# Attention and MoE on one core: a seven-product second matmul in another form, shared sums on VectorE or GpSimd, 32-bit turns of K and Q, added exponentials, and a re-planned order

## The chip, the cores and the metric

The kernel runs on one core of a Trainium2 chip. The time is device microseconds of an execution; before the change, three runs gave a median of 414.13 us (413.87 to 414.46). A profile comes from one execution under the hardware profiler. Engines are named as in the profile: PE is TensorE (PEld its weight loads), DVE is VectorE, ACT is ScalarE, POOL is GpSimd, SP is the queue that issues most stores.

## The reference

```python
# q, k, v: [8 batches, 12 heads, 448 tokens, 64], fp32
scores = q @ k.T / sqrt(64)                 # per batch and head
attn = softmax(scores)
attn_out = attn @ v
# heads side by side: x is [3584 tokens, 768]
h = x @ w_in                                # w_in [768, 2048]
g = h * sigmoid(h)
out = g @ w_out                             # w_out [2048, 768], out fp32
```

All matmul operands are rounded to fp16 in SBUF; sums are fp32 in PSUM.

## The kernel before

**Tiles and units.** A unit is one batch and one group of four heads; the first batch is cut in two pieces of queries, so there are 27 units (6 for batch 0, 3 for each of the others). For each unit GpSimd's queue issues loads of K, Q and V that turn fp32 into fp16 on the way. VectorE transposes 32x32 blocks of K and Q (`turn_k`, L279; `turn_q`, L290). Even and odd halves of the head dimension are separate slices, so that each score product contracts 32 rows, and four heads stand in four row groups of the PE array side by side.

**Attention.** `scores` (L303) writes a chunk of keys for two pairs of heads into two PSUM pairs of banks, ScalarE takes the exponential into an E buffer (`expo`, L340; nine buffers). Keys are in four chunks; from the fifth unit on, two units share their last chunk, 64 rows each (`scores_rest`). `attend` (L356) multiplies E with a matrix of ones (part 0, the denominators) and with two halves of V (parts 1 and 2), four heads in four column groups side by side; for a pair of units it does three chunks of each with 128 rows, and then both units' shares of the last chunk with 64 rows, eight abreast. VectorE inverts the denominators (`inverse`, L392 to L401) and normalises (`norm`, L409) into `xT`.

**First MoE matmul.** `ffn1` (L423), 16 row blocks of six products for each batch, then tanh on ScalarE (L434) and `gate` on VectorE (L470), which gives the gated rows `G` (with `X` for one tile that spans two batches).

**Second MoE matmul.** Token tiles of 128 are taken in pairs (`qd`, 14 pairs). For 13 pairs the 2x2 block product is made from seven block products in place of eight, each of eight matmuls (`product`, L514). Combinations of `w_out` blocks are made once (`combine_w`, L460), combinations of gated rows for each pair (`combine_g`, L504, all on VectorE). Two products share a PSUM bank by accumulation; the rest of the sums are six VectorE operations and three ScalarE copies for each pair (L567 to L581). The first pair is done plainly (`plain`, L528). Results leave by `store` (L562), four DMAs for each half tile.

**Order.** Nothing is scheduled by a compiler. A planner inside the kernel (`Order`, `Op`) runs a small clock with assumed durations, and emits each engine's instructions in the order in which it started them. Each engine then works its list strictly in order; semaphores hold real dependencies. TensorE takes scores when the pace allows, weighted sums when all exponentials of a unit are there, and else items of the MoE list. GpSimd's list holds nothing but DMA issues: `od.load` appends them in a fixed sequence. Here it is at the start, after the first batch's K, Q and V:

```python
plan_w_in(0, DFF // 4)
...
plan_w_in(DFF // 2, DFF)
plan_k(1, 1)
plan_q(NB0 + 1)
plan_w_out(0)
plan_k(1, 2)
plan_q(NB0 + 2)
for hg in range(NG):
    plan_v(1, hg, hg + 1)
plan_w_out(1)
```

Until there is real work, TensorE multiplies zeros (`run_zeros`, L1077) [...].

Of the kernel before, what the change touches and what calls it, by code (L numbers as in the profile page):

```python
# [1 line left out]

# [13 lines left out]

SWITCH = 0.094
PE_OUT = 0.20
HOP = 0.10
DMA_RATE = 0.37  # L20
DMA_TAIL = 1.0

# [5 lines left out]
def act(n):  # L28
    return n * 0.000833 + 0.093


class Ring:
# [5 lines left out]
    def can(self, n, now):  # L38
        return len(self.free) >= n and heapq.nsmallest(n, self.free)[-1] <= now

    def when(self, n):
        return heapq.nsmallest(n, self.free)[-1] if len(self.free) >= n else None

    def take(self, n=1):
        for _ in range(n):
            heapq.heappop(self.free)

    def give(self, at):
        heapq.heappush(self.free, at)
# [13 lines left out]
class Op:  # L63


    def __init__(self, eng, busy, emit, deps=(), bias=0.0, tail=HOP, then=None):
        self.eng, self.busy, self.emit = eng, busy, emit
        self.deps, self.bias, self.tail, self.then = list(deps), bias, tail, then
        self.done = None
        self.half = False  # L70
# [5 lines left out]
class Order:  # L76


    def __init__(self):
        self.now = 0.0  # L80
        self.free = {"PE": 1.2, "ACT": 2.1, "DVE": 1.2, "POOL": 1.2}
        self.wait = {"ACT": [], "DVE": []}
        self.pool = []
        self.dma_free = 0.0
        self.out = []
        self.mode = None
        self.busy = {e: 0.0 for e in self.free}
# [8 lines left out]
    def start(self, op):  # L96
        self.emit(op.emit)
        self.free[op.eng] = self.now + op.busy
        self.busy[op.eng] += op.busy
        op.done = self.now + op.busy + op.tail  # L100
        if op.then:
            op.then(op.done)
# [7 lines left out]
    def load(self, mb, emit, ring=None, gate=None):  # L110
        op = Op("POOL", 0.58, emit)
        self.pool.append((op, mb, ring, gate))
        return op

    def step(self):

        soon = []
        for eng in ("ACT", "DVE"):
            if self.free[eng] > self.now:
                soon.append(self.free[eng])  # L120
                continue
            best = None
            for op in self.wait[eng]:
                at = op.ready()
                if at is None:
                    continue
                if at > self.now:
                    soon.append(at)
                elif best is None or at + op.bias < best[0]:
                    best = (at + op.bias, op)  # L130
            if best:
                self.wait[eng].remove(best[1])
                self.start(best[1])
                soon.append(self.free[eng])
        if self.free["POOL"] > self.now:
            soon.append(self.free["POOL"])
        elif self.pool:
            op, mb, ring, gate = self.pool[0]
            at = 0.0
            if ring is not None:  # L140
                at = ring.when(1)
            if at is not None and gate is not None:
                g = gate()
                at = None if g is None else max(at, g)
            if at is not None and at <= self.now:
                self.pool.pop(0)
                if ring is not None:
                    ring.take()
# [10 lines left out]
def kernel(  # L159
# [24 lines left out]
    NFF = DFF // 128  # L184
    NDC = DM // 128
    NT = 2 * S // 128
    OH = DM // 2
    PACE = 2.6
    LONE = NG + 1
    PIECES = ((0, 7), (7, TPP))  # L190
    NE, NXT = 9, 18
    NSG, NTMP, NOST = 3, 3, 6
# [11 lines left out]
    ones = const.tile([128, 32], FP16, name="ones")  # L204
    nc.vector.memset(ones, 1.0)
# [3 lines left out]
    w_out_t = const.tile([128, NFF, DM], FP16, name="w_out_t")  # L209

    rawk, rawq, KT, QT, VT, E, acc, rdn_t, xT, g_t, ost_t = ({} for _ in range(11))
    sT_t, inv_t = {}, {}
    pS_t = {}
# [4 lines left out]
    def load_k(b, hg):  # L222
        t = sb.tile([128, TPP, 2, 32], FP16, name=f"rk_{b}_{hg}", tag="rk", bufs=2)
        nc.gpsimd.dma_start(out=t, in_=group_of(k, b, hg))  # L224
        rawk[(b, hg)] = t

    def load_q(n):
        b, hg, g0, g1 = units[n]
        t = sb.tile([128, g1 - g0, 2, 32], FP16, name=f"rq_{n}", tag="rq", bufs=3)
# [3 lines left out]
    def form(b, hg):  # L233
        n = NG * b + hg
        return "lone" if n < LONE else ("low", "high")[(n - LONE) % 2]


    def load_v(b, hg0, hg1, x):
        if b not in VT:
            VT[b] = sb.tile([128, NH, NCH, D], FP16, name=f"V_{b}", tag="V", bufs=2)  # L240
        hs = slice(HG * hg0, HG * hg1)
        first, count = X_TOK[form(b, hg0)][x]
        nc.gpsimd.dma_start(  # L243
            out=VT[b][32 * x : 32 * (x + 1), hs, 0:count, :],
# [4 lines left out]

# [15 lines left out]
    def turn_k(b, hg, e):  # L265
        t = rawk[(b, hg)]
        if e == 0:
            KT[(b, hg)] = sb.tile(
                [128, 2, NCH, 4, 32], FP16, name=f"KT_{b}_{hg}", tag="KT", bufs=3
            )  # L270
        kt = KT[(b, hg)]
        toks = X_TOK[form(b, hg)]
        x = 0
        while x < 4:
            first, count = toks[x]
            y = x + 1
            while y < 4 and toks[y][1] == count:
                y += 1
            nc.vector.transpose(  # L279
                out=kt[:, e].rearrange("p c x i -> p x c i")[:, x:y, 0:count],  # L280
                in_=t[:, first : first + count * (y - x), e, :].rearrange(
# [5 lines left out]
    def turn_q(n):  # L287
        b, hg, g0, g1 = units[n]
        qt = sb.tile([128, 2, g1 - g0, 32], FP16, name=f"QT_{n}", tag="QT", bufs=3)
        nc.vector.transpose(out=qt.rearrange("p e g i -> p g e i"), in_=rawq[n])  # L290
        QT[n] = qt

    def score_banks(n, w, ys):
        for y in ys:
            pS_t[(n, w, y)] = ps.tile(
                [128, 2, 512], FP32, name=f"s_{n}_{w}_{y}", tag="s", bufs=2
            )

    def score(pS, n, c, e, h, x0, x1, p0):
        b, hg, g0, g1 = units[n]  # L300
        nq = 32 * (g1 - g0)
        at = nq * (c % per_burst(n))
        nc.tensor.matmul(  # L303
            out=pS[p0 : p0 + 32 * (x1 - x0), h % 2, at : at + nq],
            lhsT=KT[(b, hg)][32 * h : 32 * (h + 1), e, c, x0:x1, :],
            rhs=QT[n][32 * h : 32 * (h + 1), e],
            start=(e == 0),
            stop=(e == 1),
        )


    def per_burst(n):
        return 2 if units[n][0] == 0 else 1

    def scores(n, w, ys):
        score_banks(n, w, ys)
        for c in range(per_burst(n) * w, per_burst(n) * (w + 1)):
            for e in range(2):
                for y in ys:
                    for h in (2 * y, 2 * y + 1):  # L320
                        score(pS_t[(n, w, y)], n, c, e, h, 0, rows_of(n, c) // 32, 0)


    def scores_rest(n):
        score_banks(n, 3, (0, 1))
        for e in range(2):
            for h in range(HG):
                pS = pS_t[(n, 3, h // 2)]
                score(pS, n, 3, e, h, 0, 2, 0)
                score(pS, n + 1, 3, e, h, 2, 4, 64)  # L330

    def rows_of(n, c):
        return KROWS[c] if form(*units[n][:2]) == "lone" else 128

    def expo(n, w, y):
        kr = rows_of(n, w * per_burst(n))
        nk = 32 * (units[n][3] - units[n][2]) * per_burst(n)
        if (n, w) not in E:
            E[(n, w)] = sb.tile([128, HG, S], FP16, name=f"E_{n}_{w}", tag="E", bufs=NE)
        nc.scalar.activation(  # L340
            out=E[(n, w)][0:kr, 2 * y : 2 * y + 2, 0:nk],
            in_=pS_t[(n, w, y)][0:kr, :, 0:nk],
# [5 lines left out]
    def attend_mm(a, n, part, c, h, k0, k1, e, start, stop):  # L348
        b, hg, g0, g1 = units[n]
        nq = 32 * (g1 - g0)  # L350
        at = nq * (c % per_burst(n))
        if part == 0:
            w = ones[k0:k1, :]
        else:
            w = VT[b][k0:k1, HG * hg + h, c, 32 * (part - 1) : 32 * part]
        nc.tensor.matmul(  # L356
            out=a[32 * h : 32 * (h + 1), 0:nq],
            lhsT=w,
            rhs=e[k0:k1, h, at : at + nq],
            start=start,  # L360
            stop=stop,
        )

    def attend(ns, part):
        made = []
        lone = len(ns) == 1
        for n in ns:
            a = ps.tile([128, 512], FP32, name=f"a_{n}_{part}", tag="m", bufs=4)
            made.append(a)
            acc[(n, part)] = a  # L370
            for c in range(NCH if lone else NCH - 1):
                for h in range(HG):
                    attend_mm(
                        a, n, part, c, h, 0, rows_of(n, c), E[(n, c // per_burst(n))],
                        c == 0, lone and c == NCH - 1,
                    )
        if not lone:
            for h in range(HG):
                for i, n in enumerate(ns):
                    attend_mm(  # L380
                        made[i], n, part, 3, h, 64 * i, 64 * (i + 1), E[(ns[0], 3)],
                        False, True,
                    )

    def inverse(n, step):
        g0, g1 = units[n][2:]
        shape = [128, g1 - g0, 32]
        if step == 0:  # L390
            sT_t[n] = sb.tile(shape, FP32, name=f"sT_{n}", tag="sT", bufs=1)
            nc.vector.transpose(  # L392
                out=sT_t[n],
                in_=acc[(n, 0)][:, 0 : 32 * (g1 - g0)].rearrange("p (g i) -> p g i", i=32),
            )
        elif step == 1:
            inv_t[n] = sb.tile(shape[:2] + [1], FP32, name=f"inv_{n}", tag="inv", bufs=2)
            nc.vector.reciprocal(out=inv_t[n], in_=sT_t[n][:, :, 0:1])
# [760 lines left out]
```

The softmax here doesn't subtract the row's maximum and nothing guards it: scores larger than these inputs give would overflow.

## Time and profile before

| quantity | value |
|---|---|
| median of three runs | 414.13 us |
| span of the profiled execution (first to last instruction) | 414.8 us |
| its time beyond the span | not listed apart |
| PE busy | 402.2 us, 3939 matmuls |
| VectorE busy | 285.2 us |
| ScalarE busy | 233.2 us |
| GpSimd busy (DMA issues) | 95.8 us |
| moved by DMA | 34.46 MB |

The page lists busy time by engine, then the span in 40 slices of about 10 us with a digit for the busy tenth of each, then the chain of waits that ended last, then groups of instructions. A line of the timeline gives start, duration, engine, source line, operation, output and input, count, and in brackets how long the engine had idled before it and for what. Since matmuls overlap, the distance between two starts says more of PE than the duration of one.

### The profile page before, as it was taken

How to read it: one execution, taken by the hardware profiler on the slowest of the kernel's cores; microseconds unless marked ns; L12 is line 12 of the kernel's file. 1: busy time of each engine (PE TensorE's matmuls, PEld its weight loads, DVE VectorE, ACT ScalarE, POOL GpSimd, SP SyncE). 2: the span in 40 equal slices, each digit the busy share in tenths (PEclk: the TensorE clock that was granted, in tenths of full speed). 3: DMA queues.
4: the chain of work that ended last, by engine and by line, in shares of the span. 5: the costliest groups of instructions: out<-in, count | busy, mean ns of one | idle time of the engine just before them, and what ended most of it. 6: DMA issues, size and time to landing. Idle time of an engine off the chain costs nothing.

```text
span 414.8 us, 9788 instructions
## 1 busy us (share of the span) xinstructions
PE 402.2 (97%) x3939; PEld 208.0 (50%) x3939; DVE 285.2 (69%) x654; ACT 233.2 (56%) x360; POOL 95.8 (23%) x175
## 2 busy tenths in 40 slices
PE   8999999899999999999999899999999999999994
PEld 8676765344454445544445444444445444555562
DVE  3556765899868477867868838949577557684763
ACT  2987884587365794058476197476683373314410
POOL 6685374723000810053100071403000000000000
PEclk9999999999999999999999999999999999999999
DMA  6999999954313960284402294365002300032014
GB/s 102 147 169 193 203 131 210 197 79 69 50 40 92 128 92 14 60 135 77 73 3 57 72 154 72 35 109 92 1 6 51 81 19 2 22 81 54 0 45 108
DMA packets 38749, 34.46 MB, mean 83 GB/s; under 512 B 11952, under 2 KB 37936, under 8 KB 38704
## 3 DMA queue, kind: packets, MB, share of 16 engines
q0 software_dynamic: 27952, 22.82, 38.2%
q1 hardware_dynamic: 10560, 10.83, 10.3%
q8 instruction: 31, 0.51, 0.5%
q10 hardware_dynamic: 192, 0.20, 0.2%
q14 instruction: 14, 0.11, 0.1%
HBM read 45.61 MB, written 11.01 MB: 136 GB/s over the span
## 4 chain that ended last, share of the span: by engine, by line
PE 79%; DMA 10%; DVE 6%; POOL 3%; issue 1%; ACT 0%; DVEq 0%
PE h L423 32%; PE p L514 27%; PE a L356 10%; PE s L303 8%; DMA rq<-in_q_dram 6%; DMA rk<-in_k_dram 3%; PE z L1077 2%; DMA w_in_t<-in_moe_w_in_dram 1%; POOL w_in_t L254 1%; DVE sT L392 1%; DVE KT L279 1%; POOL V L243 1%; DVE QT L290 1%; DVE rdn L401 1%; DVE xT L409 1%
## 5 line engine op out<-in xcount | busy, mean ns | idle before, releaser
L340 ACT ACTIVATE E<-s 128x896 f16<-128x896 f32 (+1 forms) x172 | 148.4, 914 | 54.3 <-PE s L303 53.3
L423 PE MATMUL h<-xT,w_in_t 128*128 128x448 f16 (+1 forms) x864 | 157.5, 333 | 2.5 <-DVE xT L409 1.5
L423 PEld LDWEIGHTS <-w_in_t 128*128 128x128 f16 x864 | 79.1, 98 | 75.8 <-issue 22.0
L470 DVE SCALAR_TENSOR_TENSOR G<-th,h 128x448 f16<-128x448 f16 (+2 forms) x144 | 74.9, 530 | 55.6 <-ACT th L434 52.6
L434 ACT ACTIVATE th<-h 128x448 f16<-128x448 f32 (+1 forms) x144 | 71.5, 506 | 55.6 <-PE h L423 47.3
L243 POOL DMA_DIRECT2D V<-in_v_dram x88 | 48.6, 564 | 127.6 <-PE a L356 108.5
L303 PE MATMUL s<-QT,KT 32*128 32x448 f16 (+4 forms) x864 | 54.3, 334 | 1.7 <-ACT E L340 1.1
L514 PEld LDWEIGHTS <-G 128*128 128x128 f16 x384 | 36.5, 98 | 29.3 <-issue 5.7
L514 PEld LDWEIGHTS <-S 128*128 128x128 f16 x312 | 29.3, 98 | 23.2 <-issue 4.3
L356 PE MATMUL a<-E,V 128*32 128x448 f16 (+3 forms) x864 | 40.5, 335 | 0.0
L279 DVE STREAM_TRANSPOSE KT<-rk 128x256 f16<-128x256 f16 (+2 forms) x96 | 31.6, 377 | 12.0 <-DMA rk<-in_k_dram 10.3
L514 PE MATMUL p<-D,G 128*128 128x384 f16 x208 | 37.8, 327 | 0.0
L514 PE MATMUL p<-w_out_t,S 128*128 128x384 f16 x208 | 37.0, 327 | 0.2 <-DVE S L504 0.2
L409 DVE SCALAR_TENSOR_TENSOR xT<-a,rdn 128x448 f16<-128x448 f32 (+1 forms) x54 | 28.7, 563 | 11.1 <-PE a L356 10.8
L514 PE MATMUL p<-w_out_t,G 128*128 128x384 f16 x176 | 31.8, 327 | 1.2 <-DVE m L567 1.2
L303 PEld LDWEIGHTS <-KT 32*128 32x128 f16 (+2 forms) x864 | 17.3, 98 | 28.2 <-issue 26.9
L504 DVE TENSOR_TENSOR S<-G 128x512 f16<-128x512 f16 x70 | 25.7, 416 | 5.5 <-PE p L514 5.4
L356 PEld LDWEIGHTS <-V 128*32 128x32 f16 (+2 forms) x864 | 17.9, 95 | 22.7 <-issue 14.7
L290 DVE STREAM_TRANSPOSE QT<-rq 128x896 f16<-128x896 f16 (+1 forms) x27 | 26.5, 983 | 0.1
L224 POOL DMA_DIRECT2D rk<-in_k_dram x24 | 13.6, 566 | 51.2 <-DVE KT L279 47.6
L577 ACT COPY ost<-p 128x384 f32<-128x384 f32 x13 | 6.2, 480 | 29.3 <-PE p L514 29.3
L392 DVE STREAM_TRANSPOSE sT<-a 128x448 f32<-128x448 f32 (+1 forms) x27 | 15.6, 579 | 9.6 <-PE a L356 9.6
(38 smaller groups left out, 252.0 us busy)
## 6 DMA issues: line engine op xcount, KB each, us to landing
out_dram<-ost SPq DMA_DIRECT2D x220, 48.0 KB, 1.6
rk<-in_k_dram POOLq DMA_DIRECT2D x24, 224.0 KB, 5.3
rq<-in_q_dram POOLq DMA_DIRECT2D x21, 224.0 KB, 6.0
w_out_t<-in_moe_w_out_dram POOLq DMA_DIRECT2D x8, 384.0 KB, 9.9
V<-in_v_dram POOLq DMA_DIRECT2D x43, 64.0 KB, 4.2
V<-in_v_dram POOLq DMA_DIRECT2D x40, 48.0 KB, 4.2
w_in_t<-in_moe_w_in_dram POOLq DMA_DIRECT2D x16, 96.0 KB, 4.7
w_in_t<-in_moe_w_in_dram POOLq DMA_DIRECT2D x8, 192.0 KB, 6.9
```

The costliest lines, as they stand in the source:

```text
L243: nc.gpsimd.dma_start(out=VT[b][32 * x : 32 * (x + 1), hs, 0:count, :], in_=v[b, hs].rearrange("h (i g) d -> i h g d", g=TPP)[:, :, first ...
L279: nc.vector.transpose(out=kt[:, e].rearrange("p c x i -> p x c i")[:, x:y, 0:count], in_=t[:, first : first + count * (y - x), e, :].rearr ...
L290: nc.vector.transpose(out=qt.rearrange("p e g i -> p g e i"), in_=rawq[n])
L303: nc.tensor.matmul(out=pS[p0 : p0 + 32 * (x1 - x0), h % 2, at : at + nq], lhsT=KT[(b, hg)][32 * h : 32 * (h + 1), e, c, x0:x1, :], rhs=QT[ ...
L340: nc.scalar.activation(out=E[(n, w)][0:kr, 2 * y : 2 * y + 2, 0:nk], in_=pS_t[(n, w, y)][0:kr, :, 0:nk], func=AF.Exp, scale=attn_scale,)
L356: nc.tensor.matmul(out=a[32 * h : 32 * (h + 1), 0:nq], lhsT=w, rhs=e[k0:k1, h, at : at + nq], start=start, stop=stop,)
L409: nc.vector.scalar_tensor_tensor(out=xT[(b, cc)][:, 32 * g0 : 32 * g1], in0=acc[(n, part)][:, 0:nq], scalar=0.5, in1=rdn_t[n].rearrange("p ...
L423: nc.tensor.matmul(out=h[:, 0 : t1 - t0], lhsT=w_in_t[:, cc, 128 * f : 128 * (f + 1)], rhs=xT[(b, cc)][:, t0:t1], start=(cc == 0), stop=(c ...
L434: nc.scalar.activation(out=th, in_=h_t[(b, f, t0)][:, 0 : t1 - t0], func=AF.Tanh)
L470: nc.vector.scalar_tensor_tensor(out=dst[:, f, at + lo : at + hi], in0=th_t[(b, f, t0)][:, lo - t0 : hi - t0], scalar=1.0, in1=h_t[(b, f, ...
L504: nc.vector.tensor_tensor(out=dst[:, f0:f1], in0=x[:, f0:f1], in1=y[:, f0:f1], op=op)
L514: nc.tensor.matmul(out=pr_t[(qd, BANK[m])][:, 0:OH], lhsT=w[:, f, :], rhs=W_[m][:, f, :], start=(f == 0 and BANK[m] == m), stop=(f == HF - 1),
```

## The change

- `turn_k` and `turn_q` transpose pairs of fp16 as single 32-bit elements. The two elements of a pair stay neighbours in KT and QT, and `score` reads every second element, so that even and odd head dimensions take the place of lower and upper halves.
- For a unit, the exponentials of chunks 0 and 1 may be added (`plan_esum`) by VectorE or GpSimd, in two halves, into a spare E buffer; the part with ones then has three chunks in place of four. The planner does it where three buffers are free: 18 of 27 units.
- The shared last key chunk is read with all 128 rows by each of the two units. V rows of the other unit are set to zero by a GpSimd memset (`load_v`, L328), and the ones have two further masks.
- The second MoE matmul uses another form of seven products (class `Quad`) for all 14 pairs: combinations of rows and of weights are built on one another, four of each (`plan_sums`, `plan_w_out_sums`), and each product is summed from PSUM with running results. Row combinations 3 and 4, `w_out` combinations and added exponentials may go to GpSimd ("VP": VectorE or GpSimd, as the planner finds one free). A product may be cut in parts of two matmuls between other items, and up to two pairs are open at once.
- The first MoE matmul keeps its products (`Plain`, L485): `PLAIN` is 8, the number of batches, so the class `Fold` for it isn't used. Combinations of `w_in` (`plan_w_in_sums`, tiles SI) are still made, on VectorE or GpSimd.
- Loads of `w_out` come behind those of batch 2, in two halves. Buffers are fixed tiles with an explicit allotment: Q 3 to 2, QT 3 to 2, V 2 to 1 by head group, and `t`, six tiles for denominators, partial sums and outputs.
- Pace and picks of the planner differ, so that all engines' orders do.

In the built program, GpSimd's list has a library reload (an ISA instruction) directly ahead of its first tensor operation, an addition of exponentials, behind the V loads of batch 1.

Core of the diff (`tt` is the helper at L510 that all sums go through):

```diff
-    PACE = 2.6
+    PACE = 2.3
+    DEFER, DITEM = .3, .1
+    SUMS, EKEEP, ESENG = (0, 1), 2, 'VP'
...
+    PLAIN = 8
...
+    W_OUT_AT = NG * len(PIECES) + 6
+    W_OUT_GAP = 2
+    NE, NX, NTMP, NSG, NF, NTH, NK = 9, 4, 6, 3, 1, 4, 2
...
+def pool(n):
+    return 0.12 + 0.00215 * n
...
     def load_v(b, hg0, hg1, x):
...
+        if count < NCH and x % 2 == 0:
+            nc.gpsimd.memset(V[32 * x : 32 * (x + 2), hs, NCH - 1, :], 0.0)
...
     def turn_q(n):
         b, hg, g0, g1 = units[n]
-        qt = sb.tile([128, 2, g1 - g0, 32], FP16, name=f"QT_{n}", tag="QT", bufs=3)
-        nc.vector.transpose(out=qt.rearrange("p e g i -> p g e i"), in_=rawq[n])
+        qt = sb.tile([128, (g1 - g0) * 32, 2], FP16, name=f"QT_{n}", tag="QT", bufs=NK)
+        nc.vector.transpose(
+            out=qt.rearrange("p (g i) e -> p g (i e)", i=32).bitcast(FP32),
+            in_=rawq[n].bitcast(FP32),
+        )
...
-            lhsT=KT[(b, hg)][32 * h : 32 * (h + 1), e, c, x0:x1, :],
-            rhs=QT[n][32 * h : 32 * (h + 1), e],
+            lhsT=KT[(b, hg)][32 * h : 32 * (h + 1), c, x0:x1, :, e].rearrange("p x i -> p (x i)"),
+            rhs=QT[m][32 * h : 32 * (h + 1), :, e],
...
+    def attend(n, part, a, es, sums):
...
+        chunks = [c for c in range(NCH) if part or c not in sums]
+        if part == 0 and sums:
+            chunks = [sums[0]] + chunks
+        for c in chunks:
+            rest = c == NCH - 1 and what != "lone"
...
+                if part == 0:
+                    w = ones[0:kr, ("low", "high").index(what) + 1 if rest else 0]
...
+    def tt(out, a, b, op, eng="DVE"):
+        e = nc.vector if eng == "DVE" else nc.gpsimd
+        e.tensor_tensor(out=out, in0=a, in1=b, op=op)
...
+    def plan_esum(n):
+
+        if not e_slots.can(1 + EKEEP, od.now):
+            return
+        at = sum_at[n] = e_slots.take(od.now)
...
+    def plan_w_out_sums():
+        loads = ld_wout[0] + ld_wout[1]
+        for f0 in range(0, HF, 2):
...
+            o1 = bulk(t1, b12, b11, ALU.subtract, loads, TB)
+            o2 = bulk(t2, b22, t1, ALU.subtract, [o1], TB)
+            o4 = bulk(t4, b21, t2, ALU.subtract, [o2], TB)
+            o3 = bulk(b12, b22, b12, ALU.subtract, [o1], TB)
...
+            self.ORDER = (1, 5, 2, 6, 7, 3, 4)
...
+            if m == 1:
+                ev["p1"] = od.add(
+                    Op("ANY", {"ACT": act(n), "DVE": vec(n)}, lambda e: copy(e, p, W), [op], SLOW)
+                )
+            elif m == 5:
+                add("r", r, Q, p, [op, ev["p1"]])
+            elif m == 2:
+                ev["c11"] = self.write(0, 0, W, self.w, [op], None)
+            elif m == 6:
+                add("y", W, Q, r, [op, ev["c11"]])
+            elif m == 7:
+                add("c22", r, Q, r, [op, ev["y"]])
...
+        if n == W_OUT_AT:
+            plan_w_out(0)
+        if n == W_OUT_AT + W_OUT_GAP:
+            plan_w_out(1)
```

## The prediction

> **What bounds the kernel now.** The page comes first: shares of the span, slices, chain.
>
> ```profile
> span 414.8 us, 9788 instructions
> PE 402.2 (97%) x3939; PEld 208.0 (50%) x3939; DVE 285.2 (69%) x654; ACT 233.2 (56%) x360; POOL 95.8 (23%) x175
> ...
> PE   8999999899999999999999899999999999999994
> ...
> DMA  6999999954313960284402294365002300032014
> ...
> PE 79%; DMA 10%; DVE 6%; POOL 3%; issue 1%; ACT 0%; DVEq 0%
> ```
>
> TensorE is busy in every slice and carries 79% of the last chain; DMA carries 10%, and the slices put that in the first 85 us. A busy PE need not be at its peak, so the timeline of 234 to 250 us is read next.
>
> ```profile
> 237.51 0.56 PE L303 MATMUL s<-QT,KT 32*128 32x448 f16 x8
> ...
> 238.00 2.44 PE L423 MATMUL h<-xT,w_in_t 128*128 128x448 f16 x12
> ...
> 240.37 0.56 PE L303 MATMUL s<-QT,KT 32*128 32x448 f16 x8
> ...
> 240.86 2.44 PE L423 MATMUL h<-xT,w_in_t 128*128 128x448 f16 x12
> ```
>
> Starts are 0.49 and 2.37 us apart. Eight scores are two rounds of four side by side, so 2r + c = 0.49 and 12r + c = 2.37: a round r is 0.188 us, a change of array shape c is 0.113 us. There is no other gap: after 82 us TensorE is a dense list, and only fewer rounds, fewer changes or new waits can move it. Before 82 us it does wait (PE timeline, 0 to 100 us):
>
> ```profile
> 1.03 7.93 PE L1077 MATMUL z<-zeros 128*128 128x128 f16 x91 [1.03 <-DVE zeros L207]
> ...
> 33.02 0.85 PE L423 MATMUL h<-xT,w_in_t 128*128 128x224 f16 x6 [0.64 <-DVE sT L392]
> ...
> 81.15 0.73 PE L423 MATMUL h<-xT,w_in_t 128*128 128x448 f16 x3 [1.16 <-DVE xT L409]
> 82.21 2.02 PE L423 MATMUL h<-xT,w_in_t 128*128 128x448 f16 x9 [0.34 <-DVE xT L409]
> ```
>
> The filler products on zeros last until the first scores; the idle times in that answer after the first 25 us add to some 3.3 us. Last, GpSimd's timeline, 30 to 110 us:
>
> ```profile
> 32.73 0.60 POOL L224 DMA_DIRECT2D rk<-in_k_dram  x1 [0.36 <-DMA w_in_t<-in_moe_w_in_dram]
> 34.35 0.55 POOL L230 DMA_DIRECT2D rq<-in_q_dram  x1 [1.02 <-DVE G L470]
> 35.01 0.75 POOL L259 DMA_DIRECT2D w_out_t<-in_moe_w_out_dram  x1
> ...
> 41.69 0.56 POOL L243 DMA_DIRECT2D V<-in_v_dram  x1 [1.28 <-DMA rk<-in_k_dram]
> 42.73 0.56 POOL L243 DMA_DIRECT2D V<-in_v_dram  x1 [0.48 <-DMA rq<-in_q_dram]
> ```
>
> An issue costs 0.55 us and often stands until an earlier transfer has landed. Now only issues stand behind it.
>
> **What the skill says.** The Trainium skill, "GPSIMD Engine Reference", section "Instruction dispatch": the first call into freshly loaded GpSimd code pays about 6 us of loading, with no instruction shown for it. The program after the change has such a load (a library reload) just ahead of GpSimd's first tensor operation; the trace before has neither. Its section "Elementwise — side-by-side cycle accounting" gives 2.6 cycles an element at 1.2 GHz for two inputs. "SBUF — State Buffer", section "SBUF: two separate sides": VectorE with two SBUF inputs and GpSimd hold it exclusively, and the loser waits for the whole instruction. No run here shows either yet. The same page, in "Door 1: The DMA port swizzle", has 16-byte lines that need two reads each for full rate; a step of 4 bytes makes four, so the pairwise KT and QT should stream as before.
>
> **The parts on TensorE.** Counts are from the two instruction orders.
> - Second matmul: 13 groups of 7 x 8 products and 64 plain ones are 792; now 14 x 56 = 784. Eight fewer at 0.163 us (eight start 1.31 us apart): -1.3.
> - Exponentials added: 18 of 27 units sum their first two key chunks, so 432 products with ones become 360: 18 rounds at 0.188, -3.4.
> - Last key chunk: 240 products of 64 rows ran eight abreast, 30 rounds. Now each unit reads all 128 rows (zeroed V, masked ones), four abreast, 60 rounds: +5.6.
> - Order: 240 changes between scores, weighted sums and full products, plus 35 inside the paired sums, become 252. 23 x 0.113: -2.6.
>
> Sum -1.7. First and second MoE matmul keep their shapes; first-matmul products stay 864.
>
> **The start.** K in fp16 costs 1.51 us a unit on VectorE (2 x (0.407 + 0.347)), Q 1.09. As fp32, half the elements: rows of `sT` (0.41 at 224, 0.63 at 448) give about 0.81 and 0.63. VectorE loses some 28 us in all, which hides under TensorE except before the first scores. Twelve fewer fillers at 0.06 to 0.09 us: -0.8, and no more, since the fillers stand in TensorE's queue. `w_out` moves from 35 us to behind the third batch's loads, so K and Q of batches 1 and 2 no longer queue behind it: I take 2.0 of the 3.3 us of early waits, bounds 0 and 3.3.
>
> **VectorE and ScalarE.** Sums of gate rows on VectorE: 130 become 74 at 0.418, -18 us busy by the rows' sum; sums and copies of products 78 at 0.55 become 59, -10; exponent adds 18 at 0.62 (between 0.418 at 512 and 0.945 at 1536), +11; weight sums about even, since 12 sums of `w_in` are new. ScalarE copies 43 become 39. With the turns, VectorE falls from 285 to about 241. All this lies beside TensorE: worth 0 while the list is dense; if that cover went, the next limit is ScalarE's 233.
>
> **GpSimd, the unknown.** It gets 18 exponent adds (896 elements, 1.94 us by the page's price), 38 row sums (512, 1.11), 6 `w_out` sums (768, 1.66), 20 `w_in` sums (384, 0.83; nothing ever multiplies by the SI tiles, as `PLAIN` is 8) and 20 memsets: 35 + 42 + 10 + 17 = 104 us, on top of 96. Half a span is free, but the queue is in order. Walk it: after `rq` at 34.35, in place of `w_out`, come one K, one Q and eight V issues, 10 x 0.55 and waits for landings as at 41.69 and 42.73 (say 2 us): 42.5. Then the reload, 6, then the add for the first unit of batch 1: 50.5. TensorE wants that sum where its ones part begins. Before, that part ran at 47.21; in the new order 2.2 us less work stands ahead of it and the start is 0.8 earlier: 44.2. TensorE stands for 50.5 - 44.2 = 6.3, taken as 6.0. Bounds: 0 (the reload is brief or already over) and 9 (it contends with transfers). Behind the add stand ten `w_in` sums, the second unit's add and then the third batch's K and Q loads, so the delay isn't won back. Scores, V parts and first-matmul products behind the waiting product wait with it, then ScalarE and VectorE.
>
> Second place: `w_out` sums, at about 100 us. VectorE's first one waits for the late `w_out` transfer with gates and norms queued behind; 10 on VectorE (0.54) and 6 on GpSimd alternate on one port, so they take 5.4 + 10 = 15.4 us, while TensorE has 72 second-matmul products (11.7) that use the results. I take 3.0, of the 3.7 difference, for this and all later collisions; bounds 0 and 8. 40 TensorE instructions now wait for GpSimd; each is a place for more.
>
> **Buffers and stores.** V goes from two buffers to one (freed by head group), QT and raw Q from three to two, xT from 18 tiles to 12, and stores leave from the six `t` tiles that also hold partial sums. A unit's loads have the time of a unit, about 12 us (27 units end by 351 us), and land in 4 to 6 us (page: 4.2 V, 5.3 K, 6.0 Q), so 0 if GpSimd is punctual; its lateness is priced above. Stores stay 224, of which 16 instead of 4 are issued by ScalarE at the end, beside SP's: 0, bounds ±1 with the tail.
>
> **The tail.** Products of the last two groups are contiguous in both (112); after the last, one VectorE read and the store. 0; bounds ±1.
>
> **Sum** against the profiled span: 414.8 - 1.7 - 0.8 - 2.0 + 6.0 + 3.0 = 419.3. That execution's span stands 0.7 above the median of 414.13, so 418.6. No time around the span is listed apart.
>
> **Rivals.**
> 1. GpSimd late, as above: 415.1 to 425. Chance 0.58.
> 2. Cover holds, on the other side: the first add is ready by 44.2, which asks for a reload under some 0.5 us or an earlier V issue. Then only the dense list counts: 414.8 - 4.5 - 0.7 = 409.6, up to 413.3 with small waits. For it: TensorE waits only about 1 us after 82 us now, so orders written this way are followed closely. Against: nothing that TensorE needs promptly came from GpSimd. 0.25.
> 3. The waits equal the gain (4 to 5 us): within 0.2% of 414.13. 0.07.
> 4. GpSimd or the port is a limit throughout: 36 of the 40 TensorE waits come a further 0.25 to 0.5 us late: +9 to +18, so 428 to 437. Against: half of GpSimd is free. 0.07.
> 5. The change isn't as free as it says: QT read at a step of two streams at half rate. 864 scores are 98 bursts, 74 of 448 columns with 0.38 us each and 24 of 224 with half that: another 32, 451. Against: the cacheline note. 0.03.
>
> **How the numbers follow.** A measurement of this kernel can tell 0.2%, 0.8 us, from no change. Faster is rival 2, 0.25; same is rival 3, 0.07; slower is 1, 4 and 5, 0.68. The time is that of case 1, 418.6; its own range is 415.1 to 425. The range given reaches down over case 2, to 409.5, and up to 428 for the upper bounds of the two GpSimd terms; half of case 4 and case 5 are left out.
>
> **What would show it.** Right: GpSimd idle or unshown for about 6 us before its first tensor operation, TensorE idle on GpSimd near 44 us, and from then all runs later; changes still 0.113. Wrong: TensorE's first wait on GpSimd under 1 us (case 2), or scores 0.87 us apart from what follows in place of 0.49 (case 5), or waits on GpSimd summing over 15 us after 110 us (case 4). If TensorE's rounds sum differently from -1.7, the count fails.

## The result, and the profile after

The changed kernel takes **526.31 us** (median of four runs, 525.06 to 526.99); before, on the same chip, it was 414.29. The ratio is 1.2675, interval 1.261 to 1.274. The forecast was 418.6 with a range up to 428, so 98 us lie above the range, and 75 above the longest time that any of its rivals named (451).

The page of the kernel after, the lines that answer to those shown of before:

```profile
span 523.3 us, 9760 instructions
...
PE 428.2 (82%) x3853; PEld 210.9 (40%) x3853; DVE 281.6 (54%) x565; ACT 235.6 (45%) x356; POOL 210.6 (40%) x277
...
PE   8997787977589879888788987798788777779775
...
PE 53%; DVE 17%; DMA 10%; ACT 8%; issue 7%; POOL 4%; DVEq 0%; ACTq 0%; POOLq 0%
```

TensorE does 3853 products in place of 3939 and is idle for nearly a fifth of the span. No other engine is above 54%, so none has become a limit. The slices mostly read 7 and 8, from end to end, where they read 9: the loss isn't at one place, and it goes on in the last slices, where GpSimd does little. The chain hops between PE, VectorE and ScalarE. That is the picture of engines that take turns, not of one that is late.

The waits of TensorE after (what it waited for, us in total, times, longest), five of 28 rows:

```profile
PE p L485 <- ACT th L498: 18.1, 27, 1.0
PE p L804 <- DVE t L510: 13.8, 16, 2.2
PE p L485 <- DVE G L501: 10.6, 19, 2.7
PE p L804 <- ACT t L514: 6.7, 12, 0.6
...
PE p L432 <- POOL E L510: 0.8, 1, 0.8
```

All 28 add to 89 us. Before, the same view has nine rows that add to 6.6; its first is

```profile
PE h L423 <- DVE xT L409: 1.5, 2, 1.2
```

After, GpSimd is named once, with 0.8. The waits are for tanh, gates, copies and sums, that is, for whoever *reads* PSUM. The timeline of PE near the end shows one form of it:

```profile
503.98 0.49 PE L804 MATMUL p<-w_out_t,S 128*128 128x384 f16 x2
505.12 1.14 PE L804 MATMUL p<-w_out_t,S 128*128 128x384 f16 x6 [0.65 <-DVE t L510]
506.09 0.49 PE L804 MATMUL p<-TO,G 128*128 128x384 f16 x2
507.14 1.14 PE L804 MATMUL p<-TO,G 128*128 128x384 f16 x6 [0.57 <-ACT t L514]
```

Each of these products of eight starts two matmuls, stops for 0.6 us, and does the other six. Its operands were there for the first two; a copy or a sum of 0.5 us stopped the third. In the built program, the third matmul of such a product, into the second half of tile `p_2`, waits for ScalarE's copy out of the *first* half of `p_2`. That copy belongs to another product and another bank. In the first MoE matmul (timeline of all engines) the same thing makes three engines go round in a ring (the view is cut at 439 us, within a run of matmuls):

```profile
438.73 2.05 PE L485 MATMUL p<-xT,w_in_t 128*128 128x448 f16 x10
...
439.38 0.62 DVE L501 SCALAR_TENSOR_TENSOR G<-th,p 128x448 f16<-128x448 f16 x1 [1.27 <-PE p L485]
440.04 0.54 ACT L498 ACTIVATE th<-p 128x448 f16<-128x448 f32 x1 [1.73 <-DVE G L501]
...
440.88 0.54 ACT L498 ACTIVATE th<-p 128x448 f16<-128x448 f32 x1 [0.30 <-PE p L485]
441.48 2.05 PE L485 MATMUL p<-xT,w_in_t 128*128 128x448 f16 x10 [0.69 <-ACT th L498]
```

A tanh starts where a gate of another product ends, and ten matmuls start where a tanh ends. Tanh waiting for a gate costs ScalarE 37.9 us in the whole run; the kernel before has no row of that kind:

```profile
ACT th L498 <- DVE G L501: 37.9, 22, 1.7
```

What the experiments below find behind it is one line of the change that the prediction didn't price. Before, the four banks for products, weighted sums and first-matmul rows were tiles of one bank each (tag `m`). After, all eight banks are halves of four tiles:

```diff
+    P_s = [ps.tile([128, 2, 512], FP32, name=f"p_{i}") for i in range(4)]
+
+    def bank(i):
+        return P_s[i // 2][:, i % 2]
```

In the built program the dependencies are drawn at the tile, so writing one bank waits for the readers of its neighbour.

### The profile page after: what moved, and what is told of

Its sections match the earlier page's. It is cut to its first block, busy times and chain, and to the rows that moved or that the text cites. A ratio compares the mean times of both kernels' runs of the same rounds, so it can differ in the third digit from the quotient of the medians.

```text
span 523.3 us, 9760 instructions
## 1 busy us (share of the span) xinstructions
PE 428.2 (82%) x3853; PEld 210.9 (40%) x3853; DVE 281.6 (54%) x565; ACT 235.6 (45%) x356; POOL 210.6 (40%) x277
## 4 chain that ended last, share of the span: by engine, by line
PE 53%; DVE 17%; DMA 10%; ACT 8%; issue 7%; POOL 4%; DVEq 0%; ACTq 0%; POOLq 0%
PE p L485 22%; PE p L804 21%; PE p L432 7%; ACT th L498 6%; DMA rq<-in_q_dram 5%; DVE G L501 4%; PE p L383 3%; DMA w_in_t<-in_moe_w_in_dram 2%; DVE xT L465 2%; DVE t L510 2%; DVE S L510 2%; DVE E L510 2%; DMA rk<-in_k_dram 2%; DVE t L454 2%; POOL V L329 2%
## 5 line engine op out<-in xcount | busy, mean ns | idle before, releaser
L485 PE MATMUL p<-xT,w_in_t 128*128 128x448 f16 (+1 forms) x864 | 164.3, 333 | 37.3 <-ACT th L498 18.1
L408 ACT ACTIVATE E<-p 128x896 f16<-128x896 f32 (+1 forms) x172 | 148.6, 916 | 73.1 <-PE p L383 72.2
L501 DVE SCALAR_TENSOR_TENSOR G<-th,p 128x448 f16<-128x448 f16 (+2 forms) x144 | 76.3, 535 | 104.1 <-ACT th L498 47.7
L485 PEld LDWEIGHTS <-w_in_t 128*128 128x128 f16 x864 | 82.4, 98 | 117.8 <-issue 61.0
L498 ACT ACTIVATE th<-p 128x448 f16<-128x448 f32 (+1 forms) x144 | 70.5, 502 | 109.1 <-PE p L485 47.2
L804 PE MATMUL p<-w_out_t,G 128*128 128x384 f16 x304 | 61.4, 333 | 14.1 <-DVE t L510 6.8
L510 POOL TENSOR_TENSOR G<-G 128x512 f16<-128x512 f16 x21 | 25.1, 1206 | 95.5 <-DVE S L510 95.0
L383 PE MATMUL p<-QT,KT 32*128 32x448 f16 (+4 forms) x864 | 55.9, 342 | 2.3 <-ACT E L408 2.2
L329 POOL DMA_DIRECT2D V<-in_v_dram x88 | 48.9, 563 | 14.8 <-PE p L432 11.2
L432 PE MATMUL p<-E,V 128*32 128x448 f16 (+2 forms) x864 | 44.5, 337 | 8.0 <-DVE X L501 6.0
L804 PE MATMUL p<-TO,S 128*128 128x384 f16 x192 | 40.9, 340 | 12.1 <-DVE t L454 4.3
L510 DVE TENSOR_TENSOR t<-p,t 128x384 f32<-128x384 f32 x42 | 23.3, 554 | 49.4 <-PE p L804 46.4
L510 POOL TENSOR_TENSOR E<-E,E 128x896 f16<-128x896 f16 x18 | 35.5, 1971 | 31.9 <-ACT E L408 31.7
L465 DVE SCALAR_TENSOR_TENSOR xT<-p,t 128x448 f16<-128x448 f32 (+1 forms) x54 | 30.2, 566 | 18.3 <-PE p L432 15.1
L510 POOL TENSOR_TENSOR G<-X,G 128x512 f16<-128x512 f16 x4 | 4.9, 1214 | 62.4 <-DVE S L510 62.4
```

What stands on the lines that cost most here:

```text
L329: nc.gpsimd.dma_start(out=V[32 * x : 32 * (x + 1), hs, 0:count, :], in_=v[b, hs].rearrange("h (i g) d -> i h g d", g=TPP)[:, :, first : fi ...
L383: nc.tensor.matmul(out=P_s[s_pair][p0 : p0 + 32 * (x1 - x0), h % 2, at : at + nq], lhsT=KT[(b, hg)][32 * h : 32 * (h + 1), c, x0:x1, :, e] ...
L408: nc.scalar.activation(out=E_s[e_i][0:kr, 2 * y : 2 * y + 2, 0:nk], in_=P_s[s_pair][0:kr, :, 0:nk], func=AF.Exp, scale=attn_scale,)
L432: nc.tensor.matmul(out=bank(a)[32 * h : 32 * (h + 1), 0:nq], lhsT=w, rhs=E_s[sum_at[n] if part == 0 and c in sums else es[c // per_burst(n)]][
L465: nc.vector.scalar_tensor_tensor(out=x_s[xi][:, cc % HC, 32 * g0 : 32 * g1], in0=bank(a)[:, 0:nq], scalar=0.5, in1=t_s[ti][:, 0:nq], op0=A ...
L485: nc.tensor.matmul(out=bank(a)[:, 0 : t1 - t0], lhsT=w_in_t[:, cc, 128 * f : 128 * (f + 1)], rhs=x_s[x_at[(b, cc // HC)]][:, cc % HC, t0:t ...
```

## The experiments

Each kernel derives from the changed kernel or the one before by the edit shown. The kernel before itself ran between 413.6 and 425.7 us on the later chips, so ratios are compared; a time "on the scale of 414.3" is a ratio times 414.3.

A second measure is needed for small differences, because the time follows the mean clock that TensorE was granted. The kernel before took 413.57 us at a clock of 0.998, 416.48 at 0.993, 418.99 at 0.980 and 419.95 at 0.976. A line through the 52 of its 68 runs that lie within 1.5% of the fastest, 414.4 + 255 x (1/clock - 1), leaves a scatter of 0.9 us. It is an estimate from these runs, and it assumes that the other kernels follow the clock in the same way. The experiments were not all granted the same clock, so where it matters the mean distance of a kernel from this line, over the runs that its ratio uses, is given as its excess "at equal clock". Whether GpSimd's work itself lowers the clock is not shown.

### 1. Four banks as tiles of their own (e1_own_banks)

```diff
-    P_s = [ps.tile([128, 2, 512], FP32, name=f"p_{i}") for i in range(4)]
+    P_s = [ps.tile([128, 2, 512], FP32, name=f"p_{i}") for i in range(2)]
+    M_s = [ps.tile([128, 512], FP32, name=f"m_{i}") for i in range(4)]
...
-        return P_s[i // 2][:, i % 2]
+        return P_s[i // 2][:, i % 2] if i < 4 else M_s[i - 4][:, :]
```

> The kernel after, with one edit: the four banks for products and weighted sums (4 to 7) are four tiles of one bank each, in place of the halves of two tiles of two banks; no instruction's work or place changes, only the waits drawn between instructions. Theory A (waits between the two banks of one tile: a product that goes into one bank waits for the read of its neighbour) expects most of the 112 us to vanish: 412 to 424 us. Theory B (GpSimd's results come late, as predicted) expects no change, over 500. Theory C (the chain copy, sum, sum of the new seven-product form is too long for TensorE) expects no change either, over 490.

Measured: 443.17 us, ratio 1.0588 (1.045 to 1.073), 438.7 on the scale of 414.3. Every engine's list is the one after; only where waits are drawn differs. So the two-bank tiles cost 0.209 of 414.3, **86 us of the 112** (at equal clock, 84 of 106). TensorE is busy for 93% of the span, and of tanh's waits for gates 0.6 us are left. The rest is more than was expected.

```profile
PE 409.1 (93%) x3853; PEld 209.4 (47%) x3853; DVE 286.4 (65%) x565; ACT 234.0 (53%) x356; POOL 209.4 (47%) x277
...
ACT th L499 <- DVE G L502: 0.6, 1, 0.6
```

### 2. No lending of the score banks (e2_no_lending)

Experiment 1 still has two paired tiles, which the planner lends to products when scores don't need them. Here it lends none:

```diff
     def lent():
-        if not qk_seq or silu_phase() or LEND and e_slots.when(1) is None:
-            return 0, 1, 2, 3
         return ()
```

> As e1_own_banks, and the four banks of the scores, still two tiles of two banks, are never lent to other products (the planner's order differs after the last scores and where exponential buffers run out). Theory A expects the last sharing of a tile by two products to go, so it should be as fast as e1_own_banks or faster by up to 8 us in the last 100 us: 408 to 420. Theories B and C: over 490.

Measured: ratio 1.0643 (1.054 to 1.075). No gain is seen, so nothing here lays the rest of the loss on the pairs that remain.

### 3. The kernel before with its banks paired (e3_before_paired)

```diff
+    P2 = [ps.tile([128, 2, 512], FP32, name=f"pair_{i}") for i in range(2)]
...
-        h = ps.tile([128, 512], FP32, name=f"h_{b}_{f}_{t0}", tag="m", bufs=4)
+        h = m_tile()
```

`m_tile` hands out halves of the two pairs, in the sequence of banks that the four tiles had; the same is done for weighted sums and products.

> The kernel before, every instruction and every bank as it was, but its four single-bank tiles are declared as the halves of two two-bank tiles. Theory A expects the kernel before to lose as the kernel after did: 470 to 530 us. Theories B and C expect 414.

Measured: 469.31 us in one run, 52 more than the kernel before on that chip (417.16). Its page and the first of its TensorE waits:

```profile
span 467.5 us, 9755 instructions
...
PE 414.1 (89%) x3939; PEld 211.3 (45%) x3939; DVE 285.9 (61%) x654; ACT 232.4 (50%) x360; POOL 95.8 (21%) x175
```

```profile
PE pair L435 <- DVE G L482: 8.8, 14, 1.4
```

The old kernel, with nothing else of the change, shows the same disease: TensorE falls from 97% to 89%, products wait for gates, and tanh for gates again (11.2 us, 19 times). The declaration alone costs 52 us here.

### 4. No sums on GpSimd (e4_no_gpsimd_sums)

```diff
-    SUMS, EKEEP, ESENG = (0, 1), 2, 'VP'
+    SUMS, EKEEP, ESENG = (0, 1), 2, 'DVE'
...
-    VPS = (3, 4)
-    WENG = 'VP'
+    VPS = ()
+    WENG = 'DVE'
```

On top of experiment 1, all sums are VectorE's.

> As e1_own_banks, and all tensor work that GpSimd may do is planned on VectorE (no library reload, no shared-port collisions; GpSimd issues DMAs and clears V rows). Theory A expects it within 6 us of e1_own_banks. Theory B expects this one alone to be near 415 to 440 while e1_own_banks stays over 500. Theory C: over 490.

Measured: 425.44 us, ratio 1.0229 (1.014 to 1.032), 423.8 on the scale. GpSimd's sums, with the order that the planner makes around them, cost **15 us** (438.7 to 423.8; 13 at equal clock), although VectorE now has more to do. The expectation, within 6, missed. The page:

```profile
PE 405.1 (96%) x3853; PEld 205.7 (49%) x3853; DVE 279.2 (66%) x650; ACT 232.4 (55%) x353; POOL 101.1 (24%) x195
```

### 5 to 7. Which of GpSimd's sums

Three kernels give back one kind or two: exponent adds only (e6), row and weight sums only (e7), exponent adds and row sums (e11). They differ from experiment 4 in its constants alone:

```diff
+    SUMS, EKEEP, ESENG = (0, 1), 2, 'VP'      # e6, e11
...
+    VPS = (3, 4)                              # e7, e11
+    WENG = 'VP'                               # e7
```

> The changed kernel with four one-bank tiles, where GpSimd adds exponentials (with VectorE, as planned) and nothing else; row, w_out and w_in sums are VectorE's. Known: 443 with all of GpSimd's sums, 425 with none. Theory 'exponent adds cost it' (2 us each, the product with ones waits in TensorE's list): 435 to 443. Rival 'the row and weight sums cost it' (through the port they share with VectorE): 425 to 430.

> The counterpart of e6: exponentials are added on VectorE, while row sums 3 and 4, w_out and w_in sums may go to GpSimd. Theory 'exponent adds cost it': 425 to 430. Rival 'the row and weight sums cost it': 435 to 443, with VectorE's sums of 512 elements well above 0.42 us in the mean.

> The changed kernel with one-bank tiles (443 us with all of GpSimd's sums), where the w_in and w_out sums are VectorE's and GpSimd keeps exponent adds and row sums 3 and 4. Theory 'VectorE is shut out while GpSimd runs weight sums one behind the other, up to 10 us at a stretch, and that is most of the 18 us': 429 to 434, and no VectorE sum over 4 us. Rival 'single collisions with row sums, some 38 of them, are the cost': 438 to 443.

| on GpSimd | ratio | interval | on the scale | clock of the runs | excess at equal clock |
|---|---|---|---|---|---|
| nothing (e4) | 1.0229 | 1.014 to 1.032 | 423.8 | 0.982 to 0.994 | 9 |
| exponents (e6) | 1.0364 | 1.030 to 1.043 | 429.4 | 0.978 to 0.982 | 11 |
| exponents, rows (e11) | 1.0539 | 1.045 to 1.062 | 436.6 | 0.977 to 0.988 | 20 |
| exponents, rows, weights (e1) | 1.0588 | 1.045 to 1.073 | 438.7 | 0.975 to 0.983 | 22 |
| rows, weights (e7) | 1.0754 | 1.070 to 1.081 | 445.5 | 0.962 to 0.973 | 24 |

By the ratios the exponents account for about 6 us, row sums for 7 and weight sums for 2. Of these steps only that of the row sums lies clear of the intervals. At equal clock it is 8 us, the exponents' step shrinks to 2, and the weights' step stays within the scatter. So the row sums are the one kind that is shown to cost much. That e7 is slower than e1 is not shown either: its runs had the lowest clock of all, below that of any run that the line was drawn through, and at equal clock the two agree within the scatter. The rival of e6 and e7, that row and weight sums cost it, fits both kernels; e11 lies with its own rival, single collisions, and no VectorE sum in it took more than 2.8 us. One caution on e7: its output is 5% off although its edit leaves nothing out, and why is open, so nothing rests on it alone.

What the sums do to VectorE is seen in the durations. Its additions of exponentials took 0.91 us in the mean in e7 and 1.15 in e1, against 0.615 in the kernel of e8, where GpSimd adds nothing.

How a collision looks is seen in e1. First its GpSimd timeline, then VectorE's, then PE's, at 122 us:

```profile
122.32 1.64 POOL L511 TENSOR_TENSOR TO<-w_out_t,TO 128x768 f16<-128x768 f16 x1
123.91 1.88 POOL L511 TENSOR_TENSOR E<-E,E 128x896 f16<-128x896 f16 x1
125.75 1.63 POOL L511 TENSOR_TENSOR TO<-w_out_t,TO 128x768 f16<-128x768 f16 x1
127.33 1.62 POOL L511 TENSOR_TENSOR w_out_t<-w_out_t 128x768 f16<-128x768 f16 x1
128.93 1.62 POOL L511 TENSOR_TENSOR TO<-w_out_t,TO 128x768 f16<-128x768 f16 x1
```

```profile
122.97 8.00 DVE L511 TENSOR_TENSOR w_out_t<-w_out_t 128x768 f16<-128x768 f16 x1
130.89 0.54 DVE L511 TENSOR_TENSOR TO<-w_out_t,TO 128x768 f16<-128x768 f16 x1
```

```profile
131.83 4.48 PE L805 MATMUL m<-TO,S 128*128 128x384 f16 x14 [6.72 <-DVE S L511]
```

VectorE's sum takes 8.00 us, where the same sum takes 0.55 in e4. It ends at 130.97, after the fifth GpSimd sum in a row has ended at 130.55. The sum that TensorE needs stands behind it in VectorE's list, and TensorE is idle for 6.72 us.

### 8. `w_out` at its old place (e8_w_out_early)

```diff
     plan_q(NB0 + 1)
+    plan_w_out(0)
     plan_k(1, 2)
...
         plan_v(1, hg, hg + 1)
+    plan_w_out(1)
```

On top of experiment 4; the two later calls go.

> The kernel of e4 (one-bank tiles, no tensor operation on GpSimd; 425 us) with the loads of w_out back at their old places among batch 1's loads. Theory 'most of what is left over the kernel before comes from w_out arriving late' (TensorE loses some 7 us between 100 and 150 us on w_out sums): 417 to 420, and no wait on a w_out sum over 1 us. Rival 'the w_out place is nearly free, the loss sits in the first 80 us as well': 423 to 427, the early loads giving back at the start what they save at 115 us.

Measured: ratio 1.0382 (1.032 to 1.044), 430.1 on the scale, so 6 us *slower* than with the loads late. Part of that is the clock, 0.976 to 0.992 here; at equal clock the difference is 3.6, give or take 1.4. Both theories missed: the old place isn't what the kernel lacks, and the change's move of `w_out` is worth at least the 2.0 that was taken for it.

### 9. 32-bit turns alone (e5_before_32bit_turns)

The kernel before with `turn_k`, `turn_q` and `score` as after, all lists in their old order; the second of the planner's two K turns for a unit issues nothing.

```diff
-        nc.vector.transpose(out=qt.rearrange("p e g i -> p g e i"), in_=rawq[n])
+        nc.vector.transpose(
+            out=qt.rearrange("p (g i) e -> p g (i e)", i=32).bitcast(FP32),
+            in_=rawq[n].bitcast(FP32),
+        )
```

> The kernel before with one part of the change alone: K and Q transposed as 32-bit pairs, scores reading every second fp16; every list in its old order. Theory 'the step of two is free': VectorE busy falls from 285 to about 257 us, a burst of eight scores still stands 0.49 to 0.51 us ahead of what follows, time 412 to 415 us, the same or a little faster through earlier first scores. Rival 'a step of two streams at half rate': bursts 0.87 us apart, about 450 us.

Measured: ratio 0.9995 (0.996 to 1.003). VectorE is busy 262.6 us in place of 285.2. PE's timeline:

```profile
244.91 0.57 PE L306 MATMUL s<-QT,KT 32*128 32x448 f16 x8
245.41 2.44 PE L426 MATMUL h<-xT,w_in_t 128*128 128x448 f16 x12
```

A burst is 0.50 us ahead of what follows (median 0.51), where it was 0.49; the clock of this trace was 0.982, that of before 0.998. Reading every second fp16 doesn't halve the rate, and 22.6 us off VectorE change the time by less than the interval, since TensorE didn't wait for it.

### 10. Without the sums that nothing reads (e10_no_w_in_sums)

```diff
-    plan_w_in_sums()
```

> The kernel of e4 (one-bank tiles, nothing but loads and memsets on GpSimd; 425 us) without the 32 sums of w_in blocks, whose results no product reads. Theory 'they stand in VectorE's list in the first 100 us and part of the last 9 us over the kernel before is theirs': 421 to 424. Rival 'they fill idle time only': 425 to 426.

Measured: 420.66 us, ratio 1.0102 (1.007 to 1.014), 418.5 on the scale; 5 us better than e4. Its page:

```profile
span 418.6 us, 9687 instructions
...
PE 404.2 (97%) x3849; PEld 206.0 (49%) x3849; DVE 270.9 (65%) x619; ACT 232.3 (55%) x354; POOL 101.0 (24%) x195
...
PE   8989998999999999999999999999999999999995
```

With four PSUM tiles of one bank, no sums on GpSimd and no dead work, TensorE's list is dense again, 97% as before. TensorE's waits add to 9.9 us, against 6.6 before, so 3.3 us more. The kernel is 4.2 above the one before.

### 11. Exponents added, in the kernel before (e9_before_exponents_added)

The kernel of experiment 9 with the first two chunks' exponentials of 20 units added on VectorE, into two spare tiles. To make room, raw Q, the output tiles and xT have fewer buffers.

```diff
+        nc.vector.tensor_tensor(
+            out=ES[n][:, hs], in0=E[(n, 0)][:, hs], in1=E[(n, 1)][:, hs], op=ALU.add
+        )
...
+                if some and c == 1:
+                    continue
```

> The kernel before with two parts of the change, both on its own seven-product form and single banks: 32-bit turns, and the first two key chunks of 20 units added on VectorE (two adds of 896 for each unit into two spare tiles; to make room raw Q has two buffers in place of three, out tiles five for six, xT 16 for 18). TensorE does 80 fewer products with ones, 20 rounds of 0.188 us, 3.8 us. Theory 'parts that only shorten TensorE's list and keep their cover are worth what they take out of it': 409.5 to 412 where the kernel before has 414. Rival 'VectorE's adds come late for the product with ones, and fewer buffers cost the rest': 414 to 418.

Measured: ratio 0.9975 (0.994 to 1.001), some 1.0 us of the 3.8 that TensorE's list is shorter by. At equal clock it is 2.5 us below the kernel of experiment 9, give or take 0.8, so the step probably yields most of what it takes out of the list. It was the candidate for a version that beats both kernels. It beats the changed one by far; that it beats the kernel before isn't shown by the ratio, and rests on the clock estimate.

### 12. Chains on GpSimd (e12_chains_on_gpsimd)

```diff
+    CHAIN = {10: 1, 13: 2, 16: 4, 19: 8, 22: 8, 25: 1}
...
+        nc.gpsimd.tensor_tensor(out=scr[:, 1], in0=scr[:, 0], in1=scr[:, 0], op=ALU.add)
...
+        for _ in range(CHAIN.get(n, 0)):
+            od.load(0.0, chain)
```

> The kernel before with 24 additions of 512 fp16 elements on a scratch tile added to GpSimd's list, which nothing reads: 1 behind the loads of unit 10, 2 behind 13, 4 behind 16, 8 behind 19, 8 behind 22 and 1 behind 25. Theory 'VectorE's operation with two SBUF inputs waits until GpSimd has no further ready operation': the longest VectorE sum under a chain of eight lasts 3 to 9 us, under a chain of one at most 1.7. Rival 'it waits for one instruction': no VectorE sum over 1.8 us anywhere. Time 415 to 425.

Measured: 421.8 us in one run. It settles little: under the two chains of eight, VectorE happened to have no operation with two SBUF inputs. Under the chain of two it had two sums (GpSimd's and VectorE's timeline):

```profile
92.17 2.78 POOL L622 TENSOR_TENSOR scr<-scr 128x512 f16<-128x512 f16 x2
```

```profile
91.93 3.84 DVE L460 TENSOR_TENSOR w_out_t<-w_out_t 128x1536 f16<-128x1536 f16 x2
...
189.26 1.38 DVE L470 SCALAR_TENSOR_TENSOR G<-th,h 128x448 f16<-128x448 f16 x2 [2.13 <-ACT th L434]
```

The two took 3.84 us; pairs of the same shape elsewhere take 1.82. The second line is a pair of gates under a chain of eight: 1.38, as such pairs take in the kernel before. A gate reads one of its two inputs from PSUM, and was not held.

## Why the prediction was wrong, point by point

**What failed: nothing was counted for PSUM.** The part "Buffers and stores" went through V, Q, QT, xT and the `t` tiles, all in SBUF, and gave 0; the eight banks as four tiles stood in the whole diff and got no term, and no rival had it. It measured 86 us (experiment 1), and 52 in the old kernel (experiment 3). The prediction walked one wait, for the first GpSimd sum, with all that stands behind it; the same walk for a bank would have found it: who reads it, who reads its neighbour, who writes next. The Trainium skill, "Perfetto Trace Analysis", section "Matmuls", says that independent groups should rotate through different PSUM banks so that the reading of one overlaps the matmuls of the next. The runs agree, and add that in this program the banks must also be different tiles (443 us against 526).

**GpSimd late: +6.0 from a library load.** The wait was there, the cause was not. GpSimd's timeline after, its first sum, and TensorE's first wait on it:

```profile
47.35 0.54 POOL L329 DMA_DIRECT2D V<-in_v_dram  x1 [0.62 <-DMA rq<-in_q_dram]
48.03 1.87 POOL L510 TENSOR_TENSOR E<-E,E 128x896 f16<-128x896 f16 x1
```

```profile
49.95 0.75 PE L432 MATMUL p<-E,ones 128*32 128x448 f16 x10 [0.82 <-POOL E L510]
```

The last V issue ends at 47.89, the add starts at 48.03: the load costs 0.14 us at most. The Trainium skill's 6 us ("GPSIMD Engine Reference", "Instruction dispatch") isn't seen here. The sum was ready at 49.90, close to the 50.5 of the forecast, by luck: the V issues ended 5.4 us later than the walk had them. The sign named for case 2, a first wait under 1 us, came true, but only because TensorE, held by its banks, came late itself (at 48.76, where 44.2 was forecast and 46.15 is seen in e1). In e1, with the banks apart, GpSimd's add starts at 47.77, and TensorE waits 3.2 us for it (2.2 in e6 and e11):

```profile
49.70 0.75 PE L433 MATMUL m<-E,ones 128*32 128x448 f16 x10 [3.18 <-POOL E L511]
```

So the place was right, the term was about twice too large, and what made GpSimd late was the DMA issues ahead of the add, not a load.

**Later collisions: +3.0, bounds 0 and 8.** The mechanism was right, the size was not: 15 us for all of GpSimd's sums (13 at equal clock), the wait at the first sum among them, and the row sums are the largest part. The place that the prediction named, the `w_out` sums, is where the 6.72 us of e1 lie. VectorE's busy time shows what was missed: it was to fall to 241 us and stood at 281.6, in part because its 74 row sums took 0.58 us in the mean in place of 0.418, and its 18 additions of exponentials 1.12 in place of 0.62. (The prediction's own sum for the row sums doesn't come out either: 56 fewer at 0.418 are 23 us, not 18.) The price of one GpSimd operation was good: 1.97 us measured for an exponent add (1.94 estimated), 1.16 to 1.21 for a row sum (1.11).

**Dead work.** The prediction saw that nothing reads the SI tiles and let their sums lie beside other work at 0. They cost 5 us where all 32 are VectorE's (experiment 10); what they cost in the changed kernel itself was not run apart.

**The parts on TensorE.** The price of a burst held (0.51 us against 0.49); that of a change of shape was not measured again. The -3.4 for added exponentials yields about 1.0 of 3.8 by the ratio where it was tried alone, with an interval that reaches from a loss of 0.4 to a gain of 2.5, and about 2.5 at equal clock (experiment 11). The +5.6 for the shared chunk and the -1.3 for the second matmul were not run apart. The kernel of e10, which has them all, is 4.2 above the kernel before where list and start say -2.5. Of this gap of 6.7, waits are 3.3; the rest is open.

**32-bit turns at 0.** Right, and rival 5 is refuted. The estimate of 28 us off VectorE measured 22.6.

**`w_out` later: -2.0, bounds 0 and 3.3.** Right in sign: 6 us by the ratios of experiment 8, with errors of some 5, and 3.6 at equal clock, close to the upper bound.

The steps together, on the scale of 414.3: 525.1 after, 438.7 with one-bank tiles, 423.8 without GpSimd's sums, 418.5 without dead sums. At equal clock the excess over the kernel before is 106, 22, 9 and 4.5. What is left wasn't taken apart further.

## What to carry to other kernels

Price every re-declaration of a buffer like an operation: list who reads each part, and ask whether a writer of one part now waits for a reader of another. A TensorE row split in two, with a wait of one copy's length on an engine that has nothing to do with the product, was the sign here. And before work is moved to an idle GpSimd, count not its own time but VectorE's operations with two SBUF inputs that will run beside it.

## What the hardware showed that was not expected

- A VectorE sum may be held by more than one GpSimd instruction: 8.00 us behind five of them in e1, and 9.99 at the most in e7, for operations that took 0.55 and 0.62 us where GpSimd added nothing. The Trainium skill, "SBUF — State Buffer", "SBUF: two separate sides", says that the loser is blocked for the whole instruction; here it lost several times in a row. Near 128 us of the kernel after, the same two lists took turns instead (VectorE's sums 1.9 to 2.1 us each). What decides between the two stays open.
- VectorE's gates ran under GpSimd's chains at their usual length, 1.38 us a pair, and so did its transposes (experiment 12).
- Runs of the kernel before differ by 6 us along with the granted clock (413.57 at 0.998, 419.95 at 0.976), more than several of the effects looked for.
- A score burst with a step of 4 bytes took 0.51 us in the median against 0.49 with a step of 2, which agrees with the note on 16-byte lines in the same page, "Door 1: The DMA port swizzle".
